# Recall in a transposed layout: one matmul per unit, denominators in a pass of their own, coefficients broadcast through DRAM

## The chip, the cores and the metric

The kernel runs on one core of one Trainium2 chip. The metric is device time in microseconds, the median of several executions. The engines named here are PE (TensorE, matmuls), DVE (VectorE), ACT (ScalarE), POOL (GpSimd) and SP (SyncE, which issues most of the DMAs).

## The reference, cut to what matters

The input is one sequence of 2048 rows of width 512. Branch A is an attention with a compressive memory, over 4 segments of 512 rows and 32 heads of width 16; branch B is a gated FFN; a gate per row mixes them.

```python
# A, per segment s (qs, ks, vs: [1, 32, 512, 16])
p = softmax(qs @ ks.T * scale + causal_mask);  a_dot = p @ vs
pq = phi(qs)                                   # t + 1 if t > 0 else exp(t)
num = pq @ M                                   # M: [16, 16] per head, from the segments before
den = (pq @ z)[..., None] + 1e-06              # z: [16] per head
o = g * (num / den) + (1 - g) * a_dot          # g = sigmoid(beta), one per head
pk = phi(ks);  M = M + pk.T @ vs;  z = z + pk.sum(rows)
# A ends: o @ wo.   B: ((relu(x_b @ W_gate) * (x_b @ W_up)) @ W_down), x_b = x here
gx = sigmoid((x * gate_w).sum(-1));  return gx * a + (1 - gx) * b
```

In the first segment M and z are zero, so only the segments 1, 2 and 3 *recall*: they compute `num / den`.

## The kernel before, in words

**Units.** A segment has 4 units, one for each block `c` of 128 channels, that is, 8 heads; unit `u = 4 * seg + c`. Everything is in the transposed layout (channels on partitions, 512 rows along the free dimension) up to the scores. `proj_q` and `proj_k` make QT, KTe, KTo (the even and the odd heads of K, the others zeroed), and for recall and memory `pqT` and `pkT`, the function phi of Q and K. `pkT` is turned by a transposing DMA on SP to `pK`. `proj_v` makes `Vp`, which carries a column of ones next to each head's 16 values, so that a product with it has the softmax's denominator in column 16.

**Scores and PV.** `attention` fills the 4 lower PSUM banks five times for each unit with scores (line 584, row tiles of 32 partitions, four side by side), ACT takes the exponential of all 4 banks in one instruction (L604) into one of the `RE = 7` buffers E, POOL masks it (L613). Then two groups of 16 matmuls (L626, column tiles of 32, one group for even and one for odd heads) make the PV product in two of the 4 upper, "working" banks.

**Recall.** `recall` (line 681) makes two matmuls over the 512 rows (L687), one for even and one for odd heads: the weights `mbd` are a block-diagonal matrix of 4 heads, each 16 columns of M and one of z, on 32 columns. The result has the same shape as that of PV, values in 16 columns and the denominator in the 17th.

**normalise** (line 649) is used by both, with `m = 0` for PV and `m = 1` for recall. DVE transposes both banks in blocks of 32 by 32 to a tile T with rows on the partitions (L657, two instructions), adds 1e-6 to the denominators for recall (L670), takes the reciprocal (L672), multiplies it with `grc` (L674), and multiplies the values with that coefficient (L662) into `och`. In `attention` the recall's `och` is added to that of PV (L640) and the sum transposed back to `oT` (L644), which the product with `wo` reads.

**Gates.** `gate_tasks` (line 410) makes for each segment the row sums of x * gate_w (L415), and from them `rcol = exp(z)`, the ratio gx / (1 - gx) for every row. `grc` (L449) is this ratio times, for `m = 0`, the head's 1 - g, and for `m = 1` its g; the division by the ratio's counterpart happens at the very end, when the output tile is multiplied with `ngcol` = 1 - gx (L771). For the recalling segments rcol goes through DRAM (`ratio`, L445) to come back in the layout of T (`rq`, four loads, L443).

**Memory.** `memory` (line 696) makes M and z of a segment with 64 short matmuls (L705) behind the third unit's PV, DVE adds them to `mzacc` (L721) and spreads them to the block-diagonal `mbd` (L725).

**FFN.** For each segment 14 blocks of gate and up products (L463, 4 matmuls each), ReLU on ACT (L743), the product on DVE into one of 16 buffers hT (L749), then four output tiles of 14 matmuls with `wd` and 4 with `wo`.

**What sets the order.** `Plan` is a list scheduler that runs while the program is built: each task has an engine, an assumed duration, dependencies with assumed latencies, needed buffers and a key; a free engine takes the ready task with the lowest key. The instructions are written out in order of the planned start times, one queue for each engine, and every engine then works through its queue strictly in order. `SHIFT` moves the keys of single tasks by number. `plan.link` makes PE run tasks right behind one another: the memory's matmuls follow a PV group. FFN keys lie later than attention keys (16000 against 14800 for a unit), so FFN matmuls fill PE between the attention's steps, and what is left of them runs at the end.

Of the kernel before, what the change touches and what calls it, by code (L numbers as in the profile page):

```python
# [12 lines left out]
P = 128  # L13
# [14 lines left out]
RE = 7  # L28
# [4 lines left out]
    22: -80000, 23: 130000, 38: 50000, 62: -90000, 69: -10000, 75: 10000, 80: 7000, 83: -50000,  # L33
    88: -110000, 123: 30000, 151: 30000, 170: -30000, 179: 40000, 203: 70000, 207: -10000,
    219: -230000, 222: -10000, 234: -10000, 237: -16000, 243: 4000, 246: 11000, 258: 9999,
    261: -7500, 267: -20000, 276: 20000, 279: -10000, 282: 10000, 288: 20000, 315: 26999,
    327: 19999, 339: -20000, 340: -100000, 341: -10000, 342: -70000, 343: -20000, 345: 20000,
    349: -40000, 354: -60000, 362: 2000, 366: -100000, 370: 56000, 375: -20000, 379: 40000,
    380: 20000, 393: -50000, 396: 60000, 399: 30000, 401: -4000, 404: 16000, 407: 10000,
    410: -13000, 418: 100000, 420: 70000, 446: 60000, 449: 27000, 476: 30000, 489: 110000,  # L40
    516: -30000, 521: -110000, 522: -50000, 528: -50000, 559: 33000, 562: -10000, 568: -10000,
    574: -10000, 580: -10000, 586: -10000, 595: 11000, 598: -20000, 601: -15000, 604: 7000,
    607: 10000, 610: -20000, 613: -10000, 616: -10000, 619: 9000, 625: 11000, 628: -6000,
    631: 2000, 634: -11000, 652: 40000, 676: 13000, 689: -70000, 690: -60000, 692: 30000,
    698: 40000, 699: -80000, 717: -30000, 720: -90000, 733: -50000, 736: -20000, 738: -60000,
    740: -110000, 743: 10000, 751: -30000, 757: -60000, 760: 20000, 767: -130000, 802: 60000,
    834: 22000, 906: -20000, 909: 9000, 912: 10000, 915: 10000, 921: -20000, 924: 10000,
    927: 14000, 936: 15000, 939: 30000, 945: 7000, 948: -17000, 954: -5000, 957: 16000,
    960: -5000, 963: -10000, 969: 10000, 972: -10000, 975: -6000, 978: -6000, 981: 12000,
    984: -20000, 987: 10000, 1002: 50000, 1014: 10000, 1040: -70000, 1050: -10000, 1055: -15000,  # L50
    1060: 20000, 1064: 50000, 1065: -20000, 1075: 1300, 1080: -10000, 1085: -10000, 1090: 28000,
    1096: 6000, 1242: 40000, 1245: 40000, 1257: 30000, 1284: -40000, 1305: -20000, 1362: 190000,
# [157 lines left out]
def kernel(  # L210
# [34 lines left out]
    xn = [sb([P, 4, D], BF16, f"xn{i}") for i in range(2)]  # L245
# [17 lines left out]
    mbd = [sb([P, NC, 2, 4, 32], BF16, f"mbd{i}") for i in range(2)]  # L263
    mzacc = sb([P, NC, 2, HW], F32, "mzacc")
    hT = ring([P, L], BF16, "hT", RH)
    T = ring([P, 2, L], F32, "T", 2)
# [4 lines left out]
    och = ring([P, L], BF16, "och", 4)  # L271
    cfr = ring([P, 2, 16], F32, "cfr", 4)
# [7 lines left out]
    def work():  # L280
# [4 lines left out]
                 x1=18400, g2=20400, u2=21600, g3=22800, u3=24000, d0=27700, d1=30400, o=31800, n1=33400,  # L285
                 x2=35200)
# [20 lines left out]
    def load_xn(seg):  # L307
        nc.sync.dma_start(out=xn[seg % 2][:], in_=x[seg * L:(seg + 1) * L, :].rearrange(
            "(t p) n -> p t n", p=P))
# [12 lines left out]
    got_n[0] = load_halves(xn[0], x[0:L, :], 4, "n")  # L322
# [16 lines left out]
    load_xn(1)  # L339
    got_n[1] = [arrival("n1")]  # L340
    load_xT(2)
    got_x[2] = [arrival("x2")] * NC
    plan.add("SP", 33100, -1e9, None)
# [9 lines left out]
    for j in range(4):  # L353
        nc.vector.memset(mcol_e[32 * j:32 * j + 16, :], 1.0)
    nc.vector.tensor_scalar(mcol_o[:], mcol_e[:], -1.0, 1.0, ALU.mult, ALU.add)
    bd = sb([P, NC, 8, HW], BF16, "bd")
    nc.gpsimd.memset(bd[:], 1.0)
    nc.gpsimd.affine_select(out=bd[:], in_=bd[:], compare_op=ALU.is_ge, fill=0.0, base=0,
                            pattern=[[0, NC], [-16, 8], [0, HW]], channel_multiplier=1)
    nc.gpsimd.affine_select(out=bd[:], in_=bd[:], compare_op=ALU.is_ge, fill=0.0, base=15,  # L360
                            pattern=[[0, NC], [16, 8], [0, HW]], channel_multiplier=-1)
    for i in range(2):
        nc.gpsimd.memset(Vp[i][:, :, :, DH:18], 1.0)
        nc.vector.memset(mbd[i][:], 0.0)
# [13 lines left out]
    gcat = sb([P, NC, 2, 2], F32, "gcat")  # L378
    grc = [sb([P, NC, 2, 2, 16], F32, f"grc{i}") for i in range(2)]
    zc = sb([P, NT], F32, "zc")  # L380
    rcol = sb([P, NT], F32, "rcol")
    rp1 = sb([P, NT], F32, "rp1")
    ngcol = sb([P, NT], F32, "ngcol")
    ratio = [dram.tile([4, 32, 4], F32, name=f"ratio{i}") for i in range(NSEG)]
    rq = [sb([P, 4, 4], F32, f"rq{i}") for i in range(2)]

    def head_gates():
        gb = gcat[:, :, 1, :]
        for j in range(4):
            nc.vector.tensor_copy(ebq[32 * j:32 * j + 32], eb.rearrange(  # L390
                "p (c j r) -> p j c r", j=4, r=2)[32 * j:32 * j + 32, j])
        nc.vector.tensor_scalar(gb, ebq[:], 1.0, None, ALU.add)
        nc.vector.reciprocal(gb, gb)
        nc.vector.tensor_tensor(gcat[:, :, 0, :], ebq[:], gb, ALU.mult)
# [3 lines left out]
    got_gates = plan.add("DVE", 1250, 0.0, head_gates, [got_eb], 100, lock=True)  # L398
# [11 lines left out]
    def gate_tasks(seg):  # L410
# [3 lines left out]
        for t in range(4):  # L414
            zs.append(plan.add("DVE", 690, key, lambda t=t: nc.vector.scalar_tensor_tensor(  # L415
                junk[:], xn[seg % 2][:, t, :], 1.0, gwb[:], ALU.mult, ALU.mult,
# [5 lines left out]
            rcol[:, cols], zc[:, cols], ACT.Exp), [b], ACL)  # L422

        def ng():
            nc.vector.tensor_scalar(rp1[:, cols], rcol[:, cols], 1.0, None, ALU.add)
# [3 lines left out]
        if seg == 0:  # L429
            sl, q0 = work(), sb([P, 4, 4], F32, "q0")  # L430
            d = plan.add("DVE", 90, key, lambda: nc.vector.tensor_tensor(
                q0[:], rcol[:, None, cols].to_broadcast([P, 4, 4]),
# [5 lines left out]
        else:  # L438
            src, frees = lambda: rq[seg % 2].rearrange("p b t -> p t b"), []

            def back():
                for j in range(4):
                    nc.sync.dma_start(out=rq[seg % 2][32 * j:32 * j + 32],  # L443
# [404 lines left out]
```

The softmax here doesn't subtract the row's maximum and nothing guards it: scores larger than these inputs give would overflow.

## Time and profile before

| what | value |
|---|---|
| median of 5 runs | 277.54 us (277.35 to 277.58) |
| profiled execution, its own time | 277.9 us |
| its span | 276.1 us |
| mean granted PE clock | 0.999 |
| PE busy, share of the span | 264.6 us, 96% |
| DVE busy | 208.3 us, 75% |
| ACT busy | 195.5 us, 71% |
| POOL busy | 86.9 us, 31% |
| DMA moved | 15.46 MB, most of it before 40 us |

In the profile's groups a line reads: line, engine, operation, output<-input, shape, count | busy us, mean ns of one | idle time of the engine just before, and what ended it. Matmuls are pipelined: the profile gives a 128x512 matmul 380 ns, though the next one starts earlier, so the time that one costs is read from the distance of starts. A DMA's time is from its issue to its landing. The releaser of a wait is inferred from the order of semaphore events.

### The profile page before, as it was taken

The page shows a single profiled execution, that of the slowest core. Times are in us where ns is not written, and L with a number is a line of the kernel's source. Part 1 is how long each engine was busy: PE and PEld are TensorE (multiplying, and loading weights), DVE is VectorE, ACT ScalarE, POOL GpSimd, SP SyncE. Part 2 cuts the span into 40 slices and gives each one's busy share as a digit, 9 for nine tenths or more (in the row PEclk, how much of TensorE's full clock was granted, in tenths as well). Part 3 has the DMA queues.
Part 4 walks back from the last instruction along what each step waited for, and adds up shares of the span by engine and source line. Part 5 has one row for each costly group of instructions (what it writes and reads, how often), then busy time and mean ns, then how long its engine had stood idle before and what let it go on. Part 6 is the DMA issues. An engine that isn't in the chain of part 4 may idle for free.

```text
span 276.1 us, 5505 instructions
## 1 busy us (share of the span) xinstructions
PE 264.6 (96%) x2175; PEld 112.7 (41%) x2211; DVE 208.3 (75%) x457; ACT 195.5 (71%) x175; POOL 86.9 (31%) x139
## 2 busy tenths in 40 slices
PE   8899999989999999999999999999999999999995
PEld 4334344343434343434344444434334434444444
DVE  5689798999999898598967992977998575464312
ACT  2189899989896777988878779689868769333000
POOL 5013243423434252424343424343334342300000
PEclk9999999999999999999999999999999999999999
DMA  6999964021311120000000100000000000000011
GB/s 221 325 238 346 276 103 151 5 40 38 58 23 38 23 40 21 0 2 19 4 0 21 40 19 2 21 0 2 0 4 0 19 29 11 21 0 0 2 38 38
DMA packets 27993, 15.46 MB, mean 56 GB/s; under 512 B 15680, under 2 KB 27968, under 8 KB 27968
## 3 DMA queue, kind: packets, MB, share of 16 engines
q1 hardware_dynamic: 26752, 14.06, 20.1%
q10 hardware_dynamic: 1216, 1.06, 1.1%
q8 instruction: 17, 0.28, 0.4%
q14 instruction: 8, 0.07, 0.1%
HBM read 9.86 MB, written 2.10 MB: 43 GB/s over the span
## 4 chain that ended last, share of the span: by engine, by line
PE 80%; DVE 9%; ACT 4%; DMA 3%; issue 3%; ACTq 0%; DVEq 0%
PE ps L463 63%; PE ps L584 8%; PE ps L626 7%; DMA wv_sb<-in_A_wv_dram 3%; PE ps L687 2%; ACT ex L511 2%; ACT E L604 1%; DVE hT L749 1%; DVE ktr L538 1%; ACT rgr L743 1%; DVE QT L522 1%; DVE och L662 1%; DVE pkT L506 1%; DVE pkT L507 1%; PE ps L705 1%
## 5 line engine op out<-in xcount | busy, mean ns | idle before, releaser
L604 ACT ACTIVATE E<-ps 128x2048 bf16<-128x2048 f32 x80 | 150.5, 1881 | 31.9 <-PE ps L584 26.2
L613 POOL TENSOR_SCALAR_AFFINE_SELECT E<-E 128x512 bf16<-128x512 bf16 x128 | 83.2, 666 | 151.2 <-ACT E L604 151.2
L463 PE MATMUL ps<-xT,wu_sb 128*128 128x512 bf16 x215 | 56.3, 380 | 0.8 <-issue 0.3
L463 PE MATMUL ps<-xT,wg_sb 128*128 128x512 bf16 x216 | 56.4, 380 | 0.6 <-issue 0.3
L463 PE MATMUL ps<-wd_sb,hT 128*128 128x512 bf16 (+1 forms) x229 | 52.8, 367 | 1.6 <-issue 1.1
L749 DVE TENSOR_TENSOR hT<-ps,rgr 128x512 bf16<-128x512 f32 x56 | 37.8, 679 | 14.4 <-PE ps L463 9.3
L743 ACT ACTIVATE rgr<-ps 128x512 bf16<-128x512 f32 x56 | 32.1, 599 | 14.1 <-PE ps L463 13.8
L657 DVE STREAM_TRANSPOSE T<-ps 128x512 f32<-128x512 f32 x56 | 37.0, 692 | 4.8 <-PE ps L626 4.3
L463 PEld LDWEIGHTS <-hT 128*128 128x128 bf16 x238 | 21.6, 98 | 25.5 <-issue 5.4
L463 PEld LDWEIGHTS <-wu_sb 128*128 128x128 bf16 x224 | 20.4, 98 | 26.1 <-issue 4.3
L463 PEld LDWEIGHTS <-wg_sb 128*128 128x128 bf16 x224 | 20.3, 98 | 26.1 <-issue 4.7
L771 DVE TENSOR_SCALAR osr<-ps,ngcol 128x512 bf16<-128x512 f32 (+1 forms) x17 | 12.2, 718 | 24.4 <-PE ps L463 24.4
L511 ACT ACTIVATE ex<-ps 128x512 bf16<-128x512 f32 x24 | 14.3, 605 | 11.6 <-DVE ktr L538 9.6
L626 PE MATMUL ps<-E,Vp 128*17 128x256 bf16 (+3 forms) x512 | 20.6, 300 | 0.7 <-DVE hT L749 0.7
L662 DVE TENSOR_TENSOR och<-T,cfr 128x512 bf16<-128x512 f32 x28 | 20.4, 736 | 0.3
L463 PE MATMUL ps<-wv_sb,xT 128*128 128x512 bf16 x62 | 16.9, 380 | 1.4 <-DMA wv_sb<-in_A_wv_dram 0.6
L584 PE MATMUL ps<-QT,KTe 32*128 32x512 bf16 (+3 forms) x256 | 17.3, 302 | 0.5 <-ACT E L604 0.4
L584 PE MATMUL ps<-QT,KTo 32*128 32x512 bf16 (+3 forms) x256 | 17.1, 299 | 0.1
L463 PE MATMUL ps<-xT,wk_sb 128*128 128x512 bf16 x60 | 16.7, 380 | 0.4 <-issue 0.2
L463 PE MATMUL ps<-wo_sb,oT 128*128 128x512 bf16 (+1 forms) x66 | 16.2, 366 | 0.2 <-issue 0.2
L463 PE MATMUL ps<-xT,wq_sb 128*128 128x512 bf16 x62 | 16.2, 380 | 0.1
L626 PEld LDWEIGHTS <-Vp 128*17 128x17 bf16 x512 | 10.8, 91 | 13.2 <-issue 3.8
(70 smaller groups left out, 189.4 us busy)
## 6 DMA issues: line engine op xcount, KB each, us to landing
out_dram<-osr SPq DMA_DIRECT2D x15, 128.0 KB, 1.7
wd_sb<-in_B_W_down_dram SPq DMA_DIRECT2D x2, 896.0 KB, 10.3
xn<-in_A_x_dram SPq DMA_DIRECT2D x3, 512.0 KB, 3.9
wg_sb<-in_B_W_gate_dram SPq DMA_DIRECT2D x2, 512.0 KB, 9.8
wu_sb<-in_B_W_up_dram SPq DMA_DIRECT2D x2, 512.0 KB, 10.0
wg_sb<-in_B_W_gate_dram SPq DMA_DIRECT2D x2, 384.0 KB, 5.0
wu_sb<-in_B_W_up_dram SPq DMA_DIRECT2D x2, 384.0 KB, 5.6
wk_sb<-in_A_wk_dram SPq DMA_DIRECT2D x1, 512.0 KB, 7.6
```

The lines of the kernel that those rows point to most:

```text
L463: nc.tensor.matmul(bank(sl)[:, 0:width], lhsT=lhsT, rhs=rhs, start=(start and q == 0), stop=(stop and q == n - 1))
L511: return es, plan.add("ACT", 478, key + 500, lambda: nc.scalar.activation(ex1[es.i][:], bank(sl), ACT.Exp), [a], ACL, need=[es], frees=[sl])
L584: nc.tensor.matmul(ps[:, j * L + off:j * L + off + n], lhsT=kt[32 * j:32 * j + 32, kb * P:(kb + 1) * P], rhs=QT[i][32 * j:32 * j + 32, kb ...
L604: nc.scalar.activation(Ef[:, e0 * L:e1 * L], ps[:, e0 * L:e1 * L], ACT.Exp, scale=SCALE),
L613: nc.gpsimd.affine_select(out=m, in_=m, compare_op=ALU.is_ge, fill=0.0, base=0, pattern=[[0, 4], [1, P]], channel_multiplier=-1)
L626: nc.tensor.matmul(bank(sl)[32 * j:32 * j + HW, kb * P:kb * P + w], lhsT=Vp[i][:, kb, 8 * c + 2 * j + r, 0:HW], rhs=E[(NFILL * u + f) % RE ...
L657: done.append(plan.add("DVE", 633, key - RL, lambda r=r, sl=sl: nc.vector.transpose(T[ts.i][:, r], bank(sl)), [a] + done, 60 if r else 0, ...
L662: nc.vector.tensor_tensor(och[ds.i].rearrange("p (q r e) -> p r q e", r=2, e=DH), t()[:, :, :, 0:DH], cfr[cs.i][:, :, :, None].to_broadcas ...
L687: a = plan.add("PE", 216, key + r, lambda r=r, sl=sl: nc.tensor.matmul(bank(sl), lhsT=mbd[i][:, c, r].rearrange("p j e -> p (j e)"), rhs=p ...
L743: r = plan.add("ACT", 478, key - RL, lambda sl=gsl, rs=rs: nc.scalar.activation(rgr[rs.i][:], bank(sl), ACT.Relu), [g], ACL, frees=[gsl])
L749: nc.vector.tensor_tensor(hT[hs1.i][:], bank(sl), rgr[rs.i][:], ALU.mult)),
L771: b = plan.add("DVE", 95 + 1.12 * w, key - RL, lambda: nc.vector.tensor_scalar(osr[os.i][:, 0:w], bank(sl)[:, 0:w], ngcol[:, tt:tt + 1], N ...
```

## The change

PV and its `normalise` stay as they are, without the `m` branch. Recall changes its layout and its arithmetic:

- **One matmul per unit.** `mbd` now holds all 8 heads of the unit on 128 columns, values only, each already multiplied with the head's g (`bdg`). The result is in the layout of `oT`: channels on partitions, rows along the free dimension.
- **Denominators apart.** `dens` (new) makes them for two units at a time: 8 matmuls of 128 columns with the weights `zbd` (z on the heads' columns), in four column tiles, one for each block of 128 rows, into one bank as [4 x 32 heads, 128 rows]. `plan.link` puts them behind a PV group. DVE adds 1e-6, takes the reciprocal of the whole 128x128 tile and multiplies it with the ratios in that layout, `rr`.
- **Coefficients through DRAM.** The result is stored to `coefs`, and for each unit loaded back as `cdr` [128, 512], the 8 heads' rows each repeated over 16 partitions. One product of the matmul's bank with `cdr` gives `omr`; it is added to `oT` after the transpose of `och`, not to `och` before it.
- **Ratios.** DVE transposes rcol in blocks of 32 (`rtp`), SP stores it as `rtok` and loads it back as `rr`. `rq` is now one load with a leading broadcast over 4 instead of four loads. `grc` has half its width.
- **Buffers.** E gets 8 instead of 7; T 1 instead of 2, och and cfr 2 instead of 4, xn 1 instead of 2. The load of the second segment's xn moves from the start into the plan. `mbd`'s two memsets on DVE give way to two of `zbd` on POOL.
- The planner's durations and latencies for these tasks and the table `SHIFT` are new, since task numbers change.

The diff, cut to its core:

```diff
-RE = 7
+RE = 8
...
-    mbd = [sb([P, NC, 2, 4, 32], BF16, f"mbd{i}") for i in range(2)]
+    mbd = [sb([P, NC, 4, 2, DH], BF16, f"mbd{i}") for i in range(2)]
+    zbd = [sb([P, NC, 4, 8], BF16, f"zbd{i}") for i in range(2)]
...
-    T = ring([P, 2, L], F32, "T", 2)
+    T = ring([P, 2, L], F32, "T", 1)
...
-    och = ring([P, L], BF16, "och", 4)
-    cfr = ring([P, 2, 16], F32, "cfr", 4)
+    och = ring([P, L], BF16, "och", 2)
+    cfr = ring([P, 2, 16], F32, "cfr", 2)
+    omr = ring([P, L], BF16, "omr", 3)
+    dnr = ring([P, P], F32, "dnr", 2)
+    cdr = ring([P, L], F32, "cdr", 3)
...
+        nc.vector.tensor_tensor(bdg[:], bd.rearrange("p c (j r) -> p c j r", r=2),
+                                gb[:, :, None, :].to_broadcast([P, NC, 4, 2]), ALU.mult)
...
-            def back():
-                for j in range(4):
-                    nc.sync.dma_start(out=rq[seg % 2][32 * j:32 * j + 32],
-                                      in_=ratio[seg].rearrange("b q t -> q b t"))
+            a = plan.add("SP", 360, key, lambda: nc.sync.dma_start(
+                out=ratio[seg].rearrange("q b t -> b q t"), in_=rcol[:, seg, 0:4]), [c], 2800)
             d = plan.add("SP", 360, key, lambda: nc.sync.dma_start(
-                out=ratio[seg].rearrange("b q t -> (b q) t"), in_=rcol[:, cols]), [c], 1700)
-            d = plan.add("SP", 1440, key, back, [d, att.get(("gate", seg - 2))], 1700)
+                out=rq[seg % 2][:], in_=ratio[seg].rearrange("q b t -> q (b t)")[None]
+                .to_broadcast([4, 32, 16])), [a, att.get(("gate", seg - 2))], 2300)
+            a = plan.add("DVE", 100, key, lambda: nc.vector.transpose(
+                rtp[seg % 2][:], rcol[:, seg]), [c], DVL)
+            a = plan.add("SP", 360, key, lambda: nc.sync.dma_start(
+                out=rtok[seg].rearrange("t b q -> b t q"), in_=rtp[seg % 2][:]), [a], 2800)
+            att["rr", seg] = plan.add("SP", 360, key, lambda: nc.sync.dma_start(
+                out=rr[seg % 2][:], in_=rtok[seg][0:4].rearrange("t b q -> t (b q)")[:, None]
+                .to_broadcast([4, 32, P])),
+                [a, att.get(("den", seg - 2, 1))], 2300)
...
+        a = plan.add("DVE", 633, key, lambda: nc.vector.transpose(
+            oT[i][:, c, :], och[oc.i][:]), [a] + war, DVL, frees=[oc])
         if seg:
             b, om = recalled[u]
             a = plan.add("DVE", 335, key, lambda: nc.vector.tensor_tensor(
-                och[oc.i][:], och[oc.i][:], och[om.i][:], ALU.add), [a, b], 110, frees=[om],
+                oT[i][:, c, :], oT[i][:, c, :], omr[om.i][:], ALU.add), [a, b], DVL, frees=[om],
                 lock=True)
...
+    def dens(seg, half):
+        i, sl, ds = seg % 2, work(), plan.one("dnr")
+        cs = [2 * half, 2 * half + 1]
+        key = KA(4 * seg + 2 * half - LEAD, -AUNIT)
+
+        def pe():
+            for k, c in enumerate(cs):
+                for t in range(4):
+                    nc.tensor.matmul(
+                        bank(sl)[32 * t:32 * t + 32, 0:P],
+                        lhsT=zbd[i][:, c].rearrange("p a h -> p (a h)"),
+                        rhs=pqT[(4 * seg + c) % RQ][:, t * P:(t + 1) * P],
+                        start=(k == 0), stop=(k == 1), tile_position=(0, 32 * t))
+        a = plan.add("PE", 120, key - PVP, pe, [prj["pq", seg, c] for c in cs]
+                     + [att["mbd", seg - 1]], PEL, need=[sl], mode="col")
+        att["denpe", seg, half] = a
+        links.setdefault(4 * seg - 1 + 2 * half, []).append(a)
+
+        def dn():
+            return dnr[ds.i][:]
+        a = plan.add("DVE", 180, key, lambda: nc.vector.tensor_scalar(
+            dn(), bank(sl)[:, 0:P], 1e-6, None, ALU.add), [a], 130, need=[ds], frees=[sl])
+        a = plan.add("DVE", 835, key, lambda: nc.vector.reciprocal(dn(), dn()), [a], 115)
+        a = plan.add("DVE", 180, key, lambda: nc.vector.tensor_tensor(
+            dn(), dn(), rr[i][:], ALU.mult), [a, att["rr", seg]], DVL, lock=True)
+        att["den", seg, half] = a
+        n = 2 * seg + half
+        att["coefs", seg, half] = plan.add("SP", 360, key, lambda: nc.sync.dma_start(
+            out=coefs[n].rearrange("h t p -> t h p"), in_=dn()), [a], 2200, frees=[ds])
+
     def recall(seg, c):
-        i, u = seg % 2, 4 * seg + c
+        i, u, sl = seg % 2, 4 * seg + c, work()
         key = KA(u - LEAD, -4000)
-        groups = []
-        for r in range(2):
-            sl = work()
-            a = plan.add("PE", 216, key + r, lambda r=r, sl=sl: nc.tensor.matmul(
-                bank(sl), lhsT=mbd[i][:, c, r].rearrange("p j e -> p (j e)"), rhs=pqT[u % RQ][:],
-                start=True, stop=True), [prj["pq", seg, c], att["mbd", seg - 1],
-                                         att["gate", seg], att.get(("comb", u - 2))],
-                PEL, need=[sl])
-            groups.append((sl, a))
+        cs, om = plan.one("cdr"), plan.one("omr")
+        n, k = 2 * seg + c // 2, c % 2
+        b = plan.add("SP", 360, key - 3000, lambda: nc.sync.dma_start(
+            out=cdr[cs.i][:], in_=coefs[n][8 * k:8 * k + 8].rearrange("h t p -> h (t p)")[:, None]
+            .to_broadcast([8, 16, L])), [att["coefs", seg, c // 2]], 2600, need=[cs])
+        a = plan.add("PE", 216, key, lambda: nc.tensor.matmul(
+            bank(sl), lhsT=mbd[i][:, c].rearrange("p j r e -> p (j r e)"), rhs=pqT[u % RQ][:],
+            start=True, stop=True), [prj["pq", seg, c], att["mbd", seg - 1], (b, 2100.0)],
+            PEL, need=[sl])
         att["recall", u] = a
-        recalled[u] = normalise(u, 1, key, groups)
+        a = plan.add("DVE", 605, key - RL, lambda: nc.vector.tensor_tensor(
+            omr[om.i][:], bank(sl), cdr[cs.i][:], ALU.mult), [a, b], DVL, need=[om],
+            frees=[sl, cs])
+        recalled[u] = a, om
...
         if seg:
             got_n[seg] = [plan.add("SP", 520, KA(4 * seg - 4), lambda seg=seg: load_xn(seg),
-                                   att.get(("xn", seg - 2), []), 3500)]
+                                   att["xn", seg - 1], 3500)]
```

## The prediction, made before the changed kernel ran

> **What bounds the kernel now.** I read four views: the busy totals and the stretches of 20 us, then the groups by line, then the order of time around a recall, then the DMA issues. First the totals and five of the stretches (start:end, length, then busy us and instruction count of PE, PEld, DVE, ACT and POOL).
>
> ```profile
> PE 264.6 (96%) x2175; PEld 112.7 (41%) x2211; DVE 208.3 (75%) x457; ACT 195.5 (71%) x175; POOL 86.9 (31%) x139
> ```
>
> ```profile
> 60.00:80.00 20.00, 19.74 (x211) 8.26 (x196) 19.18 (x46) 17.75 (x17) 6.62 (x12) 1.00 0.25 42
> 80.00:100.00 20.00, 19.08 (x150) 7.70 (x146) 18.34 (x46) 14.86 (x13) 8.51 (x14) 1.00 0.10 21
> ...
> 120.00:140.00 20.00, 19.11 (x150) 7.74 (x151) 18.26 (x40) 17.58 (x18) 7.29 (x12) 1.00 0.04 8
> ...
> 220.00:240.00 20.00, 19.73 (x165) 8.18 (x170) 10.55 (x20) 14.54 (x11) 7.70 (x13) 1.00 0.07 21
> 240.00:260.00 20.00, 19.89 (x106) 9.05 (x100) 10.82 (x18) 5.37 (x9) 0.00 (x0) 1.00 0.00 1
> ```
>
> TensorE (PE) is the bound nearly throughout: it idles 4.0 us between 60 and 240 us (180 less the nine stretches' busy time), and from 240 us on it runs the rest of the FFN without holes. So a PE instruction taken out anywhere is worth its time, as long as PE doesn't stand for something else instead. VectorE (DVE) is the second limit: 91 to 96% busy in the first three stretches shown, where PE also has its largest holes. The granted clock is 1.00, so it is no term.
>
> The groups that the change touches (last figures: busy us, mean ns of one, idle before):
>
> ```profile
> L657 DVE STREAM_TRANSPOSE T<-ps 128x512 f32<-128x512 f32 x56 | 37.0, 692 | 4.8 <-PE ps L626 4.3 <-PE ps L687 0.5
> L662 DVE TENSOR_TENSOR och<-T,cfr 128x512 bf16<-128x512 f32 x28 | 20.4, 736 | 0.3
> L672 DVE RECIPROCAL cfr<-T 128x32 f32<-128x32 f32 x28 | 9.4, 341 | 0.3
> L687 PE MATMUL ps<-pqT,mbd 128*128 128x512 bf16 x24 | 8.1, 380 | 0.7 <-ACT ex L511 0.4
> L674 DVE TENSOR_TENSOR cfr<-cfr,grc 128x32 f32<-128x32 f32 x28 | 6.5, 239 | 0.4
> ...
> L670 DVE TENSOR_SCALAR T<-T 128x32 f32<-128x32 f32 x12 | 2.0, 178 | 0.1
> ```
>
> A recall is 24 of the 128x512 matmuls. Its 380 ns is a pipelined length; the chain of waits shows what one costs:
>
> ```profile
> 241.65 10.74 PE ps L463 x49
> ```
>
> (10.74 - 0.38) / 48 = 0.216 us from one start to the next. And the order of time around one recall (start, length, engine, line):
>
> ```profile
> 122.66 0.39 PE L687 MATMUL ps<-pqT,mbd 128*128 128x512 bf16 x1
> 122.81 0.60 ACT L511 ACTIVATE ex<-ps 128x512 bf16<-128x512 f32 x1 [0.55 <-DVE ktr L538]
> ...
> 123.46 0.38 PE L687 MATMUL ps<-pqT,mbd 128*128 128x512 bf16 x1 [0.42 <-ACT ex L511]
> ```
>
> The two starts lie 0.80 us apart, 0.58 more than 0.216: the second matmul needs another bank, and that bank's reader waited for DVE. Similar holes follow recalls at 80.2 (0.27), 94.0 (0.49) and 198.0 us (0.27); the four make 1.6 us.
>
> **The change, part by part.**
>
> PE, removed: 12 of the 24 recall matmuls, 12 x 0.216 = 2.6 us, all on the bound.
>
> PE, added: six blocks of eight denominator matmuls, 128 columns each, four column tiles side by side. The nearest rows are a PV half, whose 16 matmuls stream 1280 columns four abreast in 0.55 us (170.86 to 171.41), and the memory block's 64 matmuls in 0.49 us (171.41 to 171.90). By columns a block takes 256/1280 x 0.55 = 0.11 us, by count 8/16 x 0.55 = 0.27 us; I take 0.14 because the memory block shows the array taking short matmuls every 8 ns. Six make 0.85 us (0.65 to 1.6). In the changed program's order each block stands right behind PV matmuls of the same tiling, and the changes between tilings of the array number 178 against 177, so no drain is added: 0.
>
> DVE, removed: 24 transposes (692), 12 each of the 1e-6 add (178), reciprocal (341), product with grc (239) and wide product (736): 16.6 + 17.9 = 34.5 us, and 1 us of memsets at the start. Added: 12 products omr, between 679 (hT, one operand from PSUM) and 736, say 700: 8.4; six times the block's add (298, the mzacc row of 128x136), reciprocal and product. The reciprocal takes 178 at 4 columns and 341 at 32, 5.8 ns a column, so 0.90 us at 128; the product lies between 239 (32 columns) and 468 (272), say 330: 6 x 1.53 = 9.2. Small spreads and rtp transposes, some 1.5; gates 1.1 less. DVE falls from 208 to about 191 us. By itself that is off the path and costs or brings nothing; what it can bring is the holes. I credit half of the four, -0.8 us (0 to -3.0, the last if most of the 4.0 us of idle time goes), since DVE also serves other lines there.
>
> Queues: SP issues 80 DMAs instead of 65: nine of the twelve rq reloads go, and three rtok stores, three rr loads, six coefs stores and twelve cdr loads come. Each coefs store waits for DVE, each load behind it for the store's landing, and output stores and pK transposes queue behind both. Output stores have 3 buffers and pkT has 4, so 2 to 3 us on SP are covered: 0; with the buffers used up DVE would stand at osr or pkT for the same 2 to 3 us. The second segment's xn load moves from the start to behind the first segment's row sums; it lands in 3.9 us, and its ratios first enter a product with grc, which the trace of before makes from 51.9 us on: 0, and up to 3.9 us if that cover is gone. POOL takes two early memsets more, before its first mask: 0. The rings T, och, cfr and xn shrink, but their users all run in order on DVE: 0. E grows by one buffer, which can only spare ACT some of its 5.5 us of waiting for masks: 0 on PE.
>
> The new chain is the open term: denominator matmuls, DVE, coefs to DRAM, cdr back, and omr, which holds a PSUM bank and DVE's queue until cdr has landed. The rows for landings:
>
> ```profile
> out_dram<-osr SPq DMA_DIRECT2D x15, 128.0 KB, 1.7
> xn<-in_A_x_dram SPq DMA_DIRECT2D x3, 512.0 KB, 3.9
> ...
> rq<-ratio SPq DMA_DIRECT2D x12, 2.0 KB, 1.8
> out_dram<-osr SPq DMA_DIRECT2D x2, 64.0 KB, 1.5
> ...
> ratio<-rcol SPq DMA_DIRECT2D x3, 2.0 KB, 2.4
> ```
>
> A coefs store (64 KB) lands in 1.5 to 2.4 us, say 2.0; a cdr load (256 KB) in 1.7 to 3.9, say 2.4. The shortest chain is that of the second half of the first segment that recalls (units 6 and 7): between its denominators and its first recall the new order has 28 full matmuls (6.05 us), 16 of PV (0.55) and three score fills (0.33 to 0.42 each from start to start in the order of time, and 0.1 of drain; some 1.3): 7.9 us. Behind the denominators DVE does, in order: PV half (0.65) and latency (0.2), two transposes 1.4, add 0.3, a short reciprocal 0.34, the long one 0.9, two hT 1.36, product 0.33: 5.5 us. With 2.0 + 2.4 cdr lands at 9.9 us. DVE has nine more instructions before this omr (three casts, grc and cfr products, och, KTe, a transpose, an add: 4.9 us) and reaches it at 10.4. So by the middle values nothing waits, with 0.5 us to spare. By the upper ends it lands at 5.5 + 2.4 + 3.9 = 11.8: 1.4 us of waiting. The 0.5 is less than the spread of one row's landings (rq from 1.6 to 2.9), so I charge 0.35 us at the two shortest halves (28 and 32 full matmuls): +0.7 (0 to +4.8, priced below).
>
> A rule speaks against this. The Trainium skill, "DMA: Bandwidth & Descriptors", section Rules for kernel authors, says that a DMA is spread over as many engines as its slowest dimension allows, so a leading dimension of 8 or 4 confines it to 8 or 4 of 16. The cdr loads lead with 8 heads and the coefs stores with 4 blocks. The 1.7 us row leads with 128 partitions, and no row of this trace shows a narrow one. By the rule both landings move to their upper ends and the sum would be about 2 us worse; by the rows it stays.
>
> Sum: -2.6 + 0.85 - 0.8 + 0.7 = -1.85 us. The profiled execution took 277.9 us (276.1 of span, 1.8 around it), 0.4 above the median of 277.54; I take the difference off the median: **275.7 us**.
>
> **The rivals.**
> 1. *The round trip holds VectorE (slower).* Place: the first omr of each half, six in all. At the upper ends DVE stands 1.4 us there; where DVE is over 90% busy it can't catch up, and PE, which has one working bank fewer for as long, loses what its other banks don't hold. Between nothing and 1.4 us a half I take 0.8, in all +4.8, without the credit for holes: 277.5 - 1.75 + 4.8 = 280.6 us. It decides from 1.75 / 6 = 0.3 us of PE loss per half. For it: DVE's in-order queue and the 0.5 us margin. Against: at the other halves 32 to 56 full matmuls lie between.
> 2. *Nothing moves.* PE loses its matmuls but the pace through the attention part is set by the exponentials (80 of 1881 ns), so the time comes back as waiting for scores: 277.5 us. Against: ACT itself idles 26.2 us for PE at that line, and FFN work fills PE.
> 3. *The relief is larger.* With DVE at 70% most holes between 60 and 240 us close: -1.75 - 3.0 = 272.8 us. For it: the holes sit where DVE is fullest.
>
> That the change doesn't do what it says is out: 12 recall and 48 denominator matmuls stand in its instruction order.
>
> **How the numbers follow.** Forecast 0.50, rival 3 0.12, rival 2 0.10, rival 1 0.28. Changes within 0.2% (0.55 us), about what a measurement of this kernel tells from none, are rival 2's. Faster 0.62, same 0.10, slower 0.28. The forecast's own range is 274.2 to 277.0; the full range, 273.2 to 279.4, reaches most of rival 3 and the smaller half of rival 1.
>
> **What would show it.** Right: 12 recall matmuls; denominator blocks near 0.14 us; DVE near 191 us; holes after recalls gone; omr waiting for cdr under 1 us in all; the stretch after 240 us unchanged. Wrong: DVE idle before omr put down to the cdr load, with scores or FFN matmuls late just after; or cdr landings of 3 us and more.

## The result, and the profile after

The changed kernel took **278.7 us** (median of 23 runs, 277.71 to 281.46) against 277.58 us for the kernel before (41 runs, 277.31 to 278.23). The ratio is **1.0054, 95% interval 1.0041 to 1.0066**: half a per cent slower, where 275.7 us had been forecast. (The ratio goes by the means of all runs; by the medians it is 1.0040. Ratios are used below.) The time lies inside the full range, the sign is wrong, and the first rival (the round trip holds VectorE, 280.6 us) names what happened. The profiled execution took 280.1 us, 278.1 of it span; it is one of the longer ones, and stretches are compared with that in mind.

The busy totals after (time, share of the span, instructions):

```profile
PE 263.3 (95%) x2211; PEld 112.6 (40%) x2247; DVE 192.7 (69%) x423; ACT 196.0 (70%) x175; POOL 85.0 (31%) x142
```

PE issues 2247 matmuls, as the weight loads (PEld) show; 36 of them have no record of their own, as 36 of 2211 had none before. A missing record looks like a hole. Holes of two lengths, 0.05 and 0.16 us, are common in these two traces (26 and 25 of them between 60 and 240 us, 2.7 us in all in each) and hardly occur in the kernels below whose records are complete (one or two there). Without them TensorE (PE) idles 1.2 us in that stretch before the change and 5.9 us after it, where the busy times say 4.0 and 8.6. VectorE (DVE) fell from 208.3 to 192.7 us.

The groups that the change made, with shapes kept apart:

```profile
L730 DVE TENSOR_TENSOR omr<-ps,cdr 128x512 bf16<-128x512 f32 x12 | 8.2, 688 | 7.2 <-DMA cdr<-coefs 5.5 <-PE ps L475 1.3 <-PE ps L725 0.3
L709 DVE RECIPROCAL dnr<-dnr 128x128 f32<-128x128 f32 x6 | 5.6, 926 | 0.1
L710 DVE TENSOR_TENSOR dnr<-dnr,rr 128x128 f32<-128x128 f32 x6 | 1.8, 294 | 0.0
L695 PE MATMUL ps<-pqT,zbd 128*32 128x128 bf16 x48 | 1.7, 219 | 0.0
```

The instructions cost what they were priced at. What is new is the last column of the first line: DVE stood 7.2 us in front of omr, 5.5 of it for the cdr load. The list of waits (what waited for what: us in total, times, longest) shows the same, and who waited next:

```profile
DVE omr L730 <- DMA cdr<-coefs: 5.5, 6, 1.9
...
PE ps L638 <- ACT rgr L789: 1.9, 1, 1.9
PE ps L475 <- DVE omr L730: 1.7, 4, 0.7
DVE omr L730 <- PE ps L475: 1.3, 1, 1.3
```

The last of these lines names PE, but the wait (at 112.8 to 114.1 us, below) has another likely cause: the recall matmul that feeds this omr started at 111.38, and packets of the second cdr load were still moving until 113.5. The kernel below whose omr needs no cdr (`e1_const`) has no such wait there. Counted with the others, omr waited 6.8 us.

In the chain of work that ended last, the two transfers, which were not on it before, now hold 9% of the span:

```profile
PE 63%; DMA 13%; DVE 11%; ACT 8%; issue 3%; POOL 1%; ACTq 0%; SPq 0%; DVEq 0%
PE ps L475 50%; PE ps L596 6%; ACT E L616 6%; DMA cdr<-coefs 6%; PE ps L638 6%; DMA wv_sb<-in_A_wv_dram 3%; DMA coefs<-dnr 3%; DVE omr L730 1%; DVE ktr L550 1%; ACT ex L523 1%; DMA out_dram<-osr 1%; DVE T L670 1%; POOL E L625 1%; DVE osr L817 1%; DVE hT L795 1%
```

The same chain in order of time (start, length, what), at four of the six halves:

```profile
78.66 2.45 DMA coefs<-dnr
81.13 3.65 DMA cdr<-coefs
84.90 0.69 DVE omr L730
...
104.24 2.50 DMA coefs<-dnr
106.76 4.59 DMA cdr<-coefs
111.47 0.70 DVE omr L730
...
136.80 2.48 DMA coefs<-dnr
139.30 4.17 DMA cdr<-coefs
143.56 0.70 DVE omr L730
...
168.16 3.97 DMA cdr<-coefs
```

A store lands 2.5 us after its issue, a load 3.7 to 4.6 us after. (At 168.16 it is the second load of its pair that omr waits for; it went out 1.5 us behind the first, because an output store that waited for DVE stood between them in SP's queue.) How a late load becomes idle time of PE is read in the order of time around the second half (start, length, engine, line; the wait before it in brackets):

```profile
104.24 0.56 SPq L714 DMA_DIRECT2D coefs<-dnr  x1
...
106.76 1.23 SPq L722 DMA_DIRECT2D cdr<-coefs  x2
...
111.38 0.38 PE L725 MATMUL ps<-pqT,mbd 128*128 128x512 bf16 x1
111.47 0.69 DVE L730 TENSOR_TENSOR omr<-ps,cdr 128x512 bf16<-128x512 f32 x1 [0.71 <-DMA cdr<-coefs]
...
112.21 1.89 PE L475 MATMUL ps<-xT,wg_sb 128*128 128x512 bf16 x8 [0.45 <-DVE omr L730]
...
114.10 0.69 DVE L730 TENSOR_TENSOR omr<-ps,cdr 128x512 bf16<-128x512 f32 x1 [1.34 <-PE ps L475]
...
115.37 0.68 DVE L550 CAST ktr<-ps 128x512 bf16<-128x512 f32 x1
...
116.15 0.60 ACT L523 ACTIVATE ex<-ps 128x512 bf16<-128x512 f32 x1 [2.27 <-DVE ktr L550]
...
116.64 0.59 ACT L789 ACTIVATE rgr<-ps 128x512 bf16<-128x512 f32 x1
...
117.28 0.72 PE L638 MATMUL ps<-E,Vp 128*17 128x512 bf16 x16 [1.89 <-ACT rgr L789]
```

There are two ways. The omr at 111.47 holds a PSUM bank, and the FFN matmuls behind it start 0.45 us late. The omr at 114.10 holds DVE's queue: the cast ktr behind it comes late, ACT stands 2.27 us for ktr, the ReLU rgr stands behind that in ACT's queue, and PE, whose next PV group needs rgr's bank, stands 1.89 us by the profile (0.4 us at the same place in `e1_const`). None of the three engines has to be full for that; each works its queue in order.

Four stretches show where it is lost (start:end, length, then busy us of PE, PEld, DVE, ACT, POOL; the clock stands ahead of the last two numbers). Those of the changed kernel first:

```profile
80.00:100.00 20.00, 18.40 (x137) 7.52 (x138) 15.73 (x36) 15.16 (x12) 8.06 (x13) 1.00 0.21 58
100.00:120.00 20.00, 17.29 (x227) 7.57 (x230) 14.48 (x29) 13.72 (x11) 6.65 (x11) 1.00 0.19 54
...
140.00:160.00 20.00, 18.87 (x152) 7.57 (x157) 10.81 (x23) 15.01 (x12) 7.78 (x12) 1.00 0.18 48
160.00:180.00 20.00, 18.93 (x236) 8.25 (x232) 14.99 (x33) 14.76 (x12) 6.35 (x10) 1.00 0.14 44
```

PE idles 6.5 us in these four (4.9 without the holes of missing records), and DVE is only 54 to 79% busy in them: it is late, not full.

### The profile page after: what moved, and what is told of

Same layout as the page of the kernel before. It is cut to its first block, busy times and chain, and to the rows that moved or that the text cites. A ratio compares the mean times of both kernels' runs of the same rounds, so it can differ in the third digit from the quotient of the medians.

```text
span 278.1 us, 5567 instructions
## 1 busy us (share of the span) xinstructions
PE 263.3 (95%) x2211; PEld 112.6 (40%) x2247; DVE 192.7 (69%) x423; ACT 196.0 (70%) x175; POOL 85.0 (31%) x142
## 4 chain that ended last, share of the span: by engine, by line
PE 63%; DMA 13%; DVE 11%; ACT 8%; issue 3%; POOL 1%; ACTq 0%; SPq 0%; DVEq 0%
PE ps L475 50%; PE ps L596 6%; ACT E L616 6%; DMA cdr<-coefs 6%; PE ps L638 6%; DMA wv_sb<-in_A_wv_dram 3%; DMA coefs<-dnr 3%; DVE omr L730 1%; DVE ktr L550 1%; ACT ex L523 1%; DMA out_dram<-osr 1%; DVE T L670 1%; POOL E L625 1%; DVE osr L817 1%; DVE hT L795 1%
## 5 line engine op out<-in xcount | busy, mean ns | idle before, releaser
L475 PE MATMUL ps<-xT,wg_sb 128*128 128x512 bf16 x215 | 57.0, 380 | 1.9 <-DVE omr L730 0.7
L789 ACT ACTIVATE rgr<-ps 128x512 bf16<-128x512 f32 x56 | 32.7, 604 | 14.3 <-PE ps L475 12.9
L670 DVE STREAM_TRANSPOSE T<-ps 128x512 f32<-128x512 f32 x32 | 20.9, 689 | 6.3 <-PE ps L638 6.3
L638 PE MATMUL ps<-E,Vp 128*17 128x256 bf16 (+3 forms) x512 | 21.4, 300 | 2.5 <-ACT rgr L789 1.9
L475 PE MATMUL ps<-xT,wq_sb 128*128 128x512 bf16 x63 | 16.9, 382 | 0.2 <-issue 0.2
L550 DVE CAST ktr<-ps 128x512 bf16<-128x512 f32 x16 | 11.0, 687 | 6.0 <-ACT ex L523 3.1
```

The costliest lines, as they stand in the source:

```text
L475: nc.tensor.matmul(bank(sl)[:, 0:width], lhsT=lhsT, rhs=rhs, start=(start and q == 0), stop=(stop and q == n - 1))
L550: d = plan.add("DVE", 600, key - RQK, lambda: nc.vector.tensor_copy(ktr[ks.i][:], bank(sl)), [a], DVL + 40, need=[ks], frees=[sl])
L638: nc.tensor.matmul(bank(sl)[32 * j:32 * j + HW, kb * P:kb * P + w], lhsT=Vp[i][:, kb, 8 * c + 2 * j + r, 0:HW], rhs=E[(NFILL * u + f) % RE ...
L670: done.append(plan.add("DVE", 633, key - RL, lambda r=r, sl=sl: nc.vector.transpose(T[ts.i][:, r], bank(sl)), [a] + done, 75 if r else 0, ...
L789: r = plan.add("ACT", 478, key - RL, lambda sl=gsl, rs=rs: nc.scalar.activation(rgr[rs.i][:], bank(sl), ACT.Relu), [g], ACL, frees=[gsl])
```

## The experiments

The theory after reading the trace: the change itself saves about 2 us of PE, and the late cdr loads give back more, because DVE stands for them. Each kernel changes one thing against the changed kernel or, from the fourth experiment on, against the one with bf16 coefficients.

### No wait for the coefficients, with and without the transfers

`e1_const` multiplies by a constant in place of the coefficient, so omr no longer waits; stores and loads still run. `e1_noload` drops the transfers as well.

```diff
-            omr[om.i][:], bank(sl), cdr[cs.i][:], ALU.mult), [a, b], DVL, need=[om],
+            omr[om.i][:], bank(sl), cone[:].to_broadcast([P, L]), ALU.mult), [a, b], DVL, need=[om],
```

> Leaves out the coefficient: omr multiplies the recall's bank with a constant 1, so omr waits for no landing; the stores and loads are still made, in the same order on every engine. Theory A (the landing of the loads holds VectorE's queue and a PSUM bank): VectorE's 5.5 us of waiting for the load go, and with them most of the 4.6 us by which PE's idle time from 60 to 240 us grew (8.6 against 4.0 us): 274.0 to 276.0 us, ratio to before 0.987 to 0.995. Rival B (the new order of the instructions and the smaller rings are worse by themselves, the waits only sit where PE would stand anyway): 277.8 to 279 us, ratio 1.001 to 1.006. Rival C (the traffic and SP's queue, that is late output stores and transposes, not omr's wait): no change against the changed kernel, about 278.5 us.

> As the run with the constant, and also without the six coefs stores and twelve cdr loads (left out), the instruction order otherwise the same. Theory A: equal to the run with the constant within 0.2%. Rival B: 277.8 to 279 us. Rival C: 1 us or more faster than the run with the constant, 274 to 276 us, and the output stores' waits of VectorE (1.3 us at osr) gone.

Measured: 275.46 us, ratio 0.9931 (0.9920 to 0.9943), and 275.50 us, ratio 0.9934 (0.9922 to 0.9946). So the whole loss is the wait: without it the program is 1.9 us faster than before. The 18 DMAs that `e1_noload` drops and SP's queue, with 10.5 us of SP standing for the six coefs landings, cost nothing that these runs show (0.04 us).

### The width of the load

`e1_wide` doubles each head's column in `zbd`, so that a load leads with 16 rows of 8 copies instead of 8 rows of 16 copies; the bytes stay. `e1_narrow` makes each load as two DMAs that lead with 4.

```diff
-            out=cdr[cs.i][:], in_=coefs[n][8 * k:8 * k + 8].rearrange("h t p -> h (t p)")[:, None]
-            .to_broadcast([8, 16, L])), [att["coefs", seg, c // 2]], 2600, need=[cs])
+            out=cdr[cs.i][:], in_=coefs[n][16 * k:16 * k + 16].rearrange("h t p -> h (t p)")[:, None]
+            .to_broadcast([16, 8, L])), [att["coefs", seg, c // 2]], 2600, need=[cs])
```

> Computes the same. Each head gets two columns of zbd, so that coefs holds each row twice and the load leads with 16 rows of 8 copies instead of 8 rows of 16; bytes and packets are the same, two small zbd products more per segment on VectorE (about 0.2 us each). Theory A with a load that is slow because it is spread over 8 of 16 DMA engines: the pair of loads, which now moves in 3.0 to 5.4 us, moves in about half, the first load lands 1 to 1.5 us earlier, omr's 5.5 us of waiting fall to 1 to 2.5, and the time to 275.5 to 277.3 us (ratio 0.993 to 0.999). If the width doesn't matter (the time is the round trip's fixed part): within 0.2% of the changed kernel, 278.2 to 279.2 us. Rival B: 278 to 279 us.

> Computes the same. Each load is cut in two DMAs of 4 heads each: 24 loads that lead with 4 rows instead of 12 that lead with 8. Theory A with the width: a pair of loads moves in about double the time, the waits for cdr grow by 1.5 to 3 us at each half, 12 us or more in all, and the time to 281 to 288 us (ratio 1.013 to 1.038). If only the fixed part counts: SP's extra issues of about 0.6 us each cost 0 to 1 us, 278.5 to 279.8 us. Rival B or C: under 280 us.

Measured: wide 277.29 us, ratio 0.9990 (0.9977 to 1.0002); narrow 288.19 us, ratio 1.0384 (1.0370 to 1.0397). From its first packet to the end of its last, a pair of loads (256 packets of 2 KB, of which the median one took 84 to 94 ns in all three) took 5.5 to 6.3 us when leading with 4, 3.0 to 5.4 with 8, and 2.1 to 3.9 with 16. The waits of the wide kernel:

```profile
DVE omr L730 <- DMA cdr<-coefs: 2.8, 4, 1.0
```

and of the narrow one:

```profile
DVE omr L734 <- DMA cdr<-coefs: 12.0, 5, 2.9
...
PE ps L475 <- DVE omr L734: 6.7, 5, 1.7
```

With the same bytes and packets, a wider leading dimension lands earlier, and the time follows the landing. (The narrow kernel also issues each load as two DMAs, so some of its later landing can be SP's issuing, about 0.6 us for one DMA.) Other traffic plays a part: in three halves an output store of 128 KB moves at the same time, and there a pair took 3.8 to 5.4 us with 8 rows and 2.5 to 3.9 with 16, in the other three 3.0 to 3.7 and 2.1 to 2.2.

### Half the bytes

`e2_half` keeps the 8-wide load and makes the coefficients bf16 from the last product on; `e2_wide_half` is that with 16 rows.

```diff
+    dnb = [sb([P, P], BF16, f"dnb{i}") for i in range(2)]
-    cdr = ring([P, L], F32, "cdr", 3)
+    cdr = ring([P, L], BF16, "cdr", 3)
...
-    coefs = [dram.tile([32, 4, P], F32, name=f"coefs{i}") for i in range(2 * NSEG)]
+    coefs = [dram.tile([32, 4, P], BF16, name=f"coefs{i}") for i in range(2 * NSEG)]
...
-            dn(), dn(), rr[i][:], ALU.mult), [a, att["rr", seg]], DVL, lock=True)
+            dnb[ds.i][:], dn(), rr[i][:], ALU.mult), [a, att["rr", seg]], DVL, lock=True)
```

> Computes the same with the coefficients in bf16: the last product of dens writes a bf16 tile, and coefs and cdr are bf16, so a store carries 32 KB and a load 128 KB, still on 8 rows of 16 copies. If the load's time is that of its bytes on 8 engines (theory A, width): a pair moves in 1.7 to 3 us instead of 3.0 to 5.4, the waits for cdr fall from 5.5 to 1.5 to 3 us, and the time to 276.5 to 277.7 us, as the run with 16 rows. If it is the number of packets that counts (256 for a pair in all these kernels): as the changed kernel, 278 to 279.2 us.

> Both: 16 rows of 8 copies, and bf16. The pair moves in 1.2 to 2 us, the first load lands about 1 us earlier than with 16 rows alone; waits for cdr 0 to 1.2 us; 275.5 to 276.6 us, ratio to before 0.993 to 0.997, close to the 275.5 us of the run that waits for nothing. If something else than the loads' width and bytes is left (the round trip's fixed 2.5 us of the store and about 1.5 us of the load): no better than 277 us.

Measured: **275.71 us** (275.36 to 275.79), ratio **0.9929 (0.9916 to 0.9943)**, and 275.98 us, ratio 0.9941 (0.9928 to 0.9953). The first is faster than both kernels, and leaves nothing out; its coefficients are rounded to bf16. A pair of loads (256 packets of 1 KB, 46 ns the median one) now moves in 1.6 to 1.7 us in the halves where no other packets of 1 KB move beside it, and no omr waits for cdr. Sixteen rows shorten the pair only to 1.4 to 1.5 us, which nothing waits for, and cost two more small products per segment. The stretches of `e2_half`, as above:

```profile
80.00:100.00 20.00, 19.33 (x146) 7.77 (x145) 15.68 (x35) 15.26 (x13) 8.94 (x14) 1.00 0.17 42
100.00:120.00 20.00, 19.61 (x244) 8.37 (x243) 17.13 (x36) 15.59 (x12) 6.57 (x11) 1.00 0.14 40
140.00:160.00 20.00, 19.95 (x183) 8.10 (x184) 12.13 (x26) 14.63 (x9) 7.54 (x12) 1.00 0.10 21
160.00:180.00 20.00, 20.00 (x222) 8.31 (x215) 15.02 (x32) 16.51 (x14) 7.59 (x13) 1.00 0.10 30
```

PE's idle time in the four falls from 6.5 to 1.1 us. The records are complete here and not in the changed kernel; without the holes of missing records its idle time is 4.9 us, so 3.8 us go. The spans differ by 278.1 - 273.3 = 4.8 us in these profiled executions, so most of the difference between the kernels lies in these stretches.

### Putting the matmuls back

`e3_pe` issues each recall matmul of `e2_half` twice.

```diff
-        a = plan.add("PE", 216, key, lambda: nc.tensor.matmul(
-            bank(sl), lhsT=mbd[i][:, c].rearrange("p j r e -> p (j r e)"), rhs=pqT[u % RQ][:],
-            start=True, stop=True), [prj["pq", seg, c], att["mbd", seg - 1], (b, 2100.0)],
+        def twice():
+            for _ in range(2):
+                nc.tensor.matmul(
+                    bank(sl), lhsT=mbd[i][:, c].rearrange("p j r e -> p (j r e)"),
+                    rhs=pqT[u % RQ][:], start=True, stop=True)
+        a = plan.add("PE", 216, key, twice, [prj["pq", seg, c], att["mbd", seg - 1], (b, 2100.0)],
```

> The kernel with bf16 coefficients (275.71 us), in which every recall matmul is issued twice into the same bank; the result stays the same. This puts 12 x 0.216 = 2.6 us of matmuls back on TensorE and nothing on any other engine. Theory (TensorE's instructions are the bound, so what is saved on them is worth its full time): 275.7 + 2.6 = 278.3 us, 278.0 to 278.6, ratio to before 1.002 to 1.004. Rival (the 1.9 us came from VectorE's relief or from a better order, and TensorE has slack behind a recall): 275.7 to 276.5.

Measured: 277.80 us, ratio 1.0012 (1.0003 to 1.0020). Against `e2_half` that is 2.1 us by the medians, 0.0083 x 277.5 = 2.3 us by the ratios, and 2.7 by the profiled spans (276.0 and 273.3), for 2.6 us of matmuls. It lies just under the interval of the theory and far from the rival's: what a matmul added here costs is about its full time.

### Making VectorE late on purpose

`e3_dve` put VectorE's relief back: three additions into an unused tile behind every omr. The planner's durations were left alone, so the order of all queues stayed.

```diff
+        def more():
+            nc.vector.tensor_tensor(omr[om.i][:], bank(sl), cdr[cs.i][:], ALU.mult)
+            for _ in range(3):
+                nc.vector.tensor_tensor(junk[:], omr[om.i][:], omr[om.i][:], ALU.add)
```

> The kernel with bf16 coefficients (275.71 us), with three additions of 128x512 bf16 into an unused tile behind each of the 12 products omr; the result stays the same. The oT additions of this shape take 0.50 us, so 36 of them put about 18 us back on VectorE, which is what the change had taken off it (208 to 192), in the places where the old normalisation of recall stood. Theory (VectorE's relief brought nothing; the gain is TensorE's matmuls alone): 275.6 to 276.2 us. Rival (the relief closed holes on TensorE, as the term of -0.8 us in the prediction has it): 276.5 us, and up to 278 if all that was gained goes.

Measured: 287.73 us, ratio 1.0380 (1.0347 to 1.0412): a miss for both readings, by nearly 10 us or more. VectorE is about as busy as before the change (208.9 us against 208.3), yet the time is 10 us longer. The kernel before had these 18 us in an order planned for them; here each 1.5 us is a delay that no queue was arranged around. So the run doesn't answer what it was made for, the worth of relief, but it measures what a late VectorE costs at an omr. Two smaller doses followed that up: one addition behind each omr (`e4_one`), and three behind the first omr of each half only (`e4_first`), which is about where and as long as the changed kernel waits.

```diff
-            for _ in range(3):
+            for _ in range(3 if c % 2 == 0 else 0):
```

> The kernel with bf16 coefficients, one addition of 128x512 bf16 (0.49 us) behind each of the 12 products omr instead of three: VectorE is 0.49 us late 12 times, 5.9 us in all. If TensorE's loss goes with the sum of the delays, as three additions had it (17.7 us of additions, 12.0 us of time: 0.68 us per us): 275.7 + 4.0 = 279.7 us. If each recall has a cover of its own, as large as the 0.5 us of margin that the prediction counted: 275.7 to 276.5 us.

> The kernel with bf16 coefficients, three additions of 128x512 bf16 (1.47 us) behind the first omr of each half only: VectorE is 1.47 us late 6 times, 8.8 us in all, about where and as long as the changed kernel waits for cdr (6.9 us in all). Theory (what costs is that VectorE is late at these six places, whatever makes it so): the same rate as the waits have, 0.5 to 0.7 us per us: 280 to 282 us. Rival (a wait of VectorE for a DMA costs in another way than work there): 276 to 278 us.

Measured: 278.90 us, ratio 1.0046 (1.0033 to 1.0059), and 280.54 us, ratio 1.0103 (1.0088 to 1.0118). The cover of some 0.5 us at each recall, which one of the two readings had, isn't there: even 0.47 us at a time costs over half its length.

### Half the bytes on a narrow load

`e4_half_narrow` is `e2_half` with two DMAs that lead with 4 for each load, as in `e1_narrow`.

> The kernel with bf16 coefficients (275.71 us), each cdr load made as two DMAs that lead with 4 heads instead of one that leads with 8; the result stays the same. Only the landing of the loads changes. The packets of 1 KB took 46 ns; a pair of loads has 256 of them, on 4 engines 64 each: 64 x 46 ns = 2.9 us and more, near the lower end of the changed kernel's pairs (3.0 to 5.4 us). Theory (the landing alone decides, the type of the numbers doesn't): omr waits for cdr again, 1 to 4 us in all, at 0.65 us of TensorE per us: 276.3 to 278.3 us. Rival (bf16 itself made the program faster, through VectorE or the store): 275.5 to 276.0, no wait.

Measured: 276.52 us, ratio 0.9961 (0.9946 to 0.9975). The wait is back, so it was the landing, not bf16 as such, that made `e2_half` fast:

```profile
DVE omr L735 <- DMA cdr<-coefs: 2.4, 3, 1.2
```

### One rate for all of them

All these kernels share one planned order and differ in how late DVE is at omr. The time lost is the ratio less that of the same kernel without delay (0.9931 with the constant, 0.9929 with bf16), times 277.5 us:

| kernel | DVE late at omr, us in all | time lost, us | us per us |
|---|---|---|---|
| half the bytes, narrow | 2.4, waiting | 0.9 | 0.37 |
| wide | 2.8, waiting | 1.6 | 0.6 |
| one addition | 5.6, working | 3.2 | 0.6 |
| the changed kernel | 6.8, waiting | 3.4 | 0.5 |
| three additions, first omr of a half | 9.0, working | 4.8 | 0.5 |
| narrow | 14.4, waiting | 12.6 | 0.9 |
| three additions everywhere | 17.7, working | 12.5 | 0.7 |

(The waits are those of each profiled execution, the times lost are means over all runs; the narrow kernel's 14.4 takes in 2.4 us at the second half, put down to PE while its loads were still moving. By the spans of the profiled executions themselves, 273.6 us with the constant and 278.1 in the changed kernel, the latter lost 4.5 us, 0.7 us per us, and the wide one 2.0 us, also 0.7.)

The two largest rows hold something else as well: TensorE's granted clock. In both kernels' profiles it fell to 0.50 for 3.4 us, from 118.4 us in the narrow kernel and from 179.1 us in `e3_dve`; PE had idled 1.9 and 3.3 us shortly before. In stretches of 20 us (the clock is the third number from the end), two of the narrow kernel and one of `e3_dve`:

```profile
100.00:120.00 20.00, 17.27 (x200) 7.00 (x199) 13.72 (x26) 13.73 (x11) 6.18 (x10) 0.96 0.16 50
120.00:140.00 20.00, 20.00 (x201) 8.16 (x189) 13.35 (x29) 16.03 (x14) 6.22 (x10) 0.95 0.04 8
...
180.00:200.00 20.00, 20.00 (x168) 7.68 (x158) 15.54 (x33) 15.87 (x13) 6.23 (x11) 0.94 0.01 3
```

The runs of `e3_dve` show about what it costs: 286.8 to 287.3 us at a mean clock of 0.993 to 0.994, 288.2 at 0.988, 289.6 and 289.7 at 0.982, so some 1.3 us for each step of 0.006. All four runs of the narrow kernel have 0.994. An estimate that takes 1.3 us off for each step leaves 11.3 us (0.8 us per us) for the narrow kernel and 10.1 us (0.6) for three additions everywhere. So a us of lateness costs 0.5 to 0.6 us where DVE works, at 5.6 us in all as at 17.7, and 0.4 to 0.8 us where it waits, with no free part that these runs show. What makes the clock fall was not tried; 1.89 us of idle time in the changed kernel's profile did not.

## Why the prediction was wrong

- **Recall matmuls, -2.6, and denominator blocks, +0.85.** Right in kind; the blocks were priced a little too high. The changed kernel's records show about 0.11 us from one block's entry to the next group, 0.66 in all, so the PE part is -1.94 us. The four kernels in which no omr waits for cdr came out 1.6 to 2.0 us faster than before, and duplicating the recall matmuls cost about their time.
- **VectorE's work, 208 to 191 us.** Right: 192.7. The omr took 688 ns for 700, the reciprocal 926 for 900, the product 294 for 330.
- **Half of the holes, -0.8.** Not found. The PE part alone explains the 1.9 us of the kernel without a wait, which leaves nothing for relief, net of what else the change costs. The 4.0 us of idle time between 60 and 240 us were misread: 2.7 us of them are holes of missing matmul records, and 1.2 us are left. `e2_half`, with complete records and DVE as much relieved, idles 2.0 us in the same stretch, so PE's idle time there did not fall at all. Whether relief by itself is worth anything was not settled; the run meant for it measured lateness instead.
- **The new chain, +0.7: the step that failed.** It measured +3.4 us (1.0054 less 0.9931); with the 1.9 us saved that is the 1.5 us by which the means differ. Three things in it were wrong:
  - *The landing of cdr, 2.4 us taken.* The first load of a pair landed 3.65 to 4.6 us after its issue, at the upper end given (3.9) and over it. The value came from rows that lead with 128 partitions (1.7 us for 128 KB, 3.9 for 512 KB), though the text itself said that no row showed a narrow transfer; bytes alone were used to place a load between them. The coefs store took 2.45 to 2.5 us for the 2.0 taken.
  - *The second load of each pair was left out.* It is issued 0.6 us behind the first and shares the moving time of the pair, 3.0 to 5.4 us. The longer of the two delays at the second half, 1.34 us against 0.71, stood at the second omr.
  - *The wait was charged to the two shortest halves.* The full matmuls between denominators and recall were taken as slack for the other four. But omr waits for cdr at five of the six halves. A likely reason, argued and not tried: the planner places an omr where its own assumed latencies (2200 and 2600 ns, plus the issue) let it go, so a landing later than assumed shows at every half, however many matmuls lie between.
- **The shortest chain itself.** Predicted: cdr 9.9 us after the denominators, DVE at omr at 10.4. In the trace the denominators start at 101.86, the store is issued 2.4 us later (5.5 predicted), cdr arrives after 9.5 us and DVE is ready after 8.9. That cdr's time was nearly right is luck: a DVE part shorter by 3.1 us and transfers longer by 2.7 us cancelled. At this half the margin went because DVE was ready 1.5 us earlier than predicted; in place of 0.5 us to spare it stood 0.71 us.
- **The rule weighed there.** The Trainium skill, "DMA: Bandwidth & Descriptors", section Rules for kernel authors, has a DMA's engines limited by its slowest dimension. The runs with leading dimensions of 4, 8 and 16 agree (5.5 to 6.3, 3.0 to 5.4, 2.1 to 3.9 us a pair). The prediction quoted it, gave it about 2 us, and went by the wide rows instead; 2 us added to the forecast would have been 277.7, and the measured 278.7 is beyond even that.
- **Queues and the tail, 0.** Right as far as tried: taking the 18 coefs and cdr transfers out changed 0.04 us, and after 240 us PE runs on as before (19.89 us busy of the next 20 in both).
- **Rival 1.** Right in mechanism, place and sign. It priced 4.8 us (0.8 a half); 3.4 us were measured, 0.57 a half against the 0.3 from which it was to decide. What spoke against it, the many matmuls between, did not hold. It deserved more than 0.28: a margin of 0.5 us stood against transfers for which no row was at hand.
- **Rivals 2 and 3.** Out: PE's matmuls were worth their time, and no kernel came near 272.8.

## What to carry to other kernels

A transfer through DRAM inside an in-order chain is priced by its own shape: its leading dimension and packets as much as its bytes, and all the loads issued together. If no row shows that shape, the far end of the bounds is the value to take, above all when the margin is smaller than the difference between the rows. And a wait on a half-idle engine is not free: in this program, with a fixed order on every queue, half or more of each us of lateness came through to the bound engine, so before work is removed from VectorE, ask what VectorE will now wait for. Shrinking the transfer (bf16 here) turned this change from a loss into a gain.

## What was not expected of the hardware

- Halving the bytes did more than doubling the width. A pair of 8-wide loads moved in 1.6 us with 1 KB packets and in 3.0 to 5.4 us with 2 KB packets, though the median packet went only from 84 to 46 ns. The 16-wide pair with 2 KB packets puts as many bytes on each leading row and still took 2.1 us and more. An output store beside the pair goes with the longest ones; what else lengthens the pairs of 2 KB packets beyond their packets' own time was not separated out.
- Work and waiting on VectorE cost TensorE much the same, 0.5 to 0.6 us per us of work and 0.4 to 0.8 per us of waiting, down to delays of 0.5 us.
- The changed kernel's 23 runs spread over 3.7 us. The two longest, 281.3 and 281.5 us, are the only ones with a granted clock of 0.994 (0.998 to 1.000 in the others); without them the spread is 2.5 us. The wide kernel's 12 runs spread over 2.0 us, the 5 runs each of `e1_const`, `e1_noload`, `e2_half` and `e2_wide_half` over 0.3 to 0.9. That a transfer's time varies from run to run is a likely reason and was not shown; the narrow kernel, which waits most, spread over only 0.6 us in 4 runs.
